# Weight combinations of q, k and v taken two neighbouring columns at a time

## The chip, the cores and the metric

The kernel runs on one core of a Trainium2 chip. The metric is the device time of one execution in microseconds (us); a kernel's time is the median of its runs. A core has TensorE (PE in the profile; PEld is its weight load), VectorE (DVE), ScalarE (ACT), GpSimd (POOL) and SyncE (SP), which here issues nearly all DMA transfers from one queue, in order.

## The reference

Two layers of attention and feed-forward run one after the other over 2048 tokens of 1024 features, with the same weights in both:

```python
x = x + attention(layernorm(x), wqkv, wo)
x = x + mlp(layernorm(x), w1, b1, w2, b2)      # and both once more

def attention(x, wqkv, wo):                     # 32 heads of 32 features
    q, k, v = split(x @ wqkv)
    idx = pos[:, None] - 2 * arange(8)          # a window of 8 tokens, every second one
    logits = sum(q * k[idx]) * scale            # positions before the start masked out
    return (softmax(logits) * v[idx]).sum() @ wo

def mlp(x, w1, b1, w2, b2):
    h = relu(x @ w1 + b1)
    return (h * h) @ w2 + b2                    # 1024 -> 3584 -> 1024
```

## The kernel before

**Tiling.** Tokens are cut into four blocks of 512 for each layer, so there are eight units, u = 0 to 7. For each unit the kernel does a LayerNorm and a transpose (SA, `ln`), the products for q, k and v (SQ or SQ7), the windowed attention on VectorE (S2), the product with wo, the residual sum and a second LayerNorm (SW), and the two products of the feed-forward (SF1, SF2). A unit's attention on VectorE runs beside matrix products of the unit before.

**Where the columns of q, k and v go.** The 1024 columns of q (and of k, and of v) are cut into eight chunks of 128. Chunk c holds columns c, c + 8, c + 16 and so on, since the attention wants each head's 32 features spread over the chunks. `SQ`, used for units 0 to 2, therefore loads its left factor (the weights) straight from the tile of wqkv with a step of eight columns (`wv[:, kd % 4, c0:D:8]`, line 710; line 715 for the few that are cut into halves of 256 tokens).

**Seven products in place of eight.** From unit 3 on, `SQ7` computes q, k and v by a scheme in which a product of two by two blocks takes seven block products and some sums in place of eight products. The blocks are halves of the 1024 input features (k), halves of the output columns (m) and halves of the 512 tokens. For each of q, k and v there are two such groups, s = 0 and 1. A group's weight blocks are chunks 4m + 2s and 4m + 2s + 1 of input half k. Three of the seven left factors are raw blocks and four are sums or differences of blocks. They are made once, in `keep_wqkv`, after unit 2 has used the raw weights (`QU = 2`), and written to device memory (`wqs`); units 3 to 7 read them from there (`seven`).

**How the left factors are made.** `raw(m, k)` is the view of one block: 4 slices of 128 input features by 2 chunks by 128 columns, 1024 elements in each partition, read with a step of eight columns. ScalarE copies three raw blocks (line 419, tiles `tr`) and VectorE makes four combinations s1 to s4 (line 424, tiles `tv`), where s2 uses s1 and s4 uses s2. Each result, a tile of 128 x 4 x 256 16-bit elements, is stored by a DMA on SP's queue (`store`). The six groups make 18 copies and 24 combinations. The same code shape without the step of eight is in `keep_w1` (line 548) for the feed-forward.

**How they are used.** `product` (lines 510 to 521) issues, for each of the two chunks a of a left factor, four matmuls of 256 tokens, whose left factor is 128 columns of the tile (line 519). The feed-forward products of `ffn1_step` call the same function. Five units with q, k and v make 42 products of 8 matmuls each, 1680 matmuls in all.

**What sets the order.** All work is first collected as operations with an engine, a price in microseconds and a priority (`Plan.add`). `Plan.schedule` then plays the execution through with these prices, and the order it finds is written out; each engine and SP's queue run their instructions in that order. A price is therefore part of the order and not of the hardware's time. An operation on 1024 elements is priced at `dve(1024, False)` = 1.14 for line 424 and `act(1024)` = 0.91 for line 419. Buffers come from pools with a fixed number of slots, so a late reader holds up a later writer.

Of the kernel before, what the change touches and what calls it, by code (L numbers as in the profile page):

```python
# [29 lines left out]
def dve(n, fast=True):  # L30
    return 0.075 + n * (0.000521 if fast else 0.00104)

def act(n):
    return 0.05 + n * 0.00084
# [171 lines left out]
class _Kernel:  # L206
# [191 lines left out]
    def keep_wqkv(self, nm, ws):  # L398

        nc, p = self.nc, self.p  # L400
        job = "k" if nm == "k" else "qv"

        def one(s):
            at = {pr: i for i, (d, pr) in enumerate(self.orderq[job]) if d == (nm, s)}

            def raw(m, k):
                return ws[k][:].rearrange("p (a b) n -> p a (b n)", a=4).rearrange("p a (n c) -> p a c n", c=8)[:, :, 4 * m + 2 * s:4 * m + 2 * s + 2, :]

            def store(pr, t, cast=None):
                i = at[pr]  # L410
                self.dma(lambda: self.wqs[job][i // 4][:, i % 4], lambda: t[:], [(t, 0)], [(("wqs", job, i // 4), i % 4)], 0.26, prio=50.0,
                         name="wqst", cast=cast, lat=4.0)

            def v4(t):
                return t[:].rearrange("p k (c n) -> p k c n", c=2)

            for pr, m, k in ((1, 0, 0), (2, 0, 1), (4, 1, 1)):
                t = Buf("2K", "tr", [128, 4, 256], BF)
                p.add("ACT", act(1024), lambda t=t, m=m, k=k: nc.scalar.copy(v4(t), raw(m, k)), [(ws[k], 0)], [(t, 0)], 30.0, name="trc")  # L419
                store(pr, t, BF)  # L420
            s1, s3, s2, s4 = t = [Buf("2K", "tv", [128, 4, 256], F16) for _ in range(4)]

            def comb(t, a, b, op, r, pr):
                p.add("DVE", dve(1024, False), lambda: nc.vector.tensor_tensor(v4(t), a(), b(), op), r, [(t, 0)], self.nxt(), name="tq")  # L424
                store(pr, t)
            comb(s1, lambda: raw(1, 0), lambda: raw(1, 1), ALU.add, [(ws[0], 0), (ws[1], 0)], 5)
            comb(s3, lambda: raw(0, 0), lambda: raw(1, 0), ALU.subtract, [(ws[0], 0)], 7)
            comb(s2, lambda: v4(s1), lambda: raw(0, 0), ALU.subtract, [(ws[0], 0), (s1, 0)], 6)
            comb(s4, lambda: raw(0, 1), lambda: v4(s2), ALU.subtract, [(ws[1], 0), (s2, 0)], 3)
        one(0)  # L430
        one(1)

    def SQ7(self, u, job):
# [36 lines left out]
    def qkv_step(self, u, nm, s):  # L470

        nc, p = self.nc, self.p
        dst = self.state[u][nm]
        off = 0 if nm == "q" else HALO
        X, Y, Z = (Buf("ps", n, [128, 2, HB], F32) for n in "XYZ")
        us = {}

        def out(m, n2):
            return dst[:, 4 * m + 2 * s:4 * m + 2 * s + 2, off + n2 * HB:off + (n2 + 1) * HB]

        def cells(m, n2):
            return [(dst, (4 * m + 2 * s + a, n2)) for a in range(2)]

        def keep(i):
            us[i] = Buf("1K", "u", [128, 2, HB], F16)
            p.add("ACT", act(512), lambda: nc.scalar.copy(us[i][:], X[:]), [(X, 0)], [(us[i], 0)], 1.0, name="u")  # L486

        def vadd(m, n2, i, bank):
            p.add("DVE", dve(512, False), lambda: nc.vector.tensor_tensor(out(m, n2), us[i][:], bank[:], ALU.add),
                  [(us[i], 0), (bank, 0)], cells(m, n2), -90.0, name="qa")  # L490

        def mul(pr, w, wi, rhs, rc):
            bank, fm = self.product(pr, w, wi, rhs, X, Y, Z)
            self.state[u]["gate" + nm] = p.add("PE", 4 * MM, fm, rc + [(w, 0)], [(bank, 0)], self.nxt(), name="fq")
            if pr == 1:
                keep(1)
            elif pr == 2:
                vadd(0, 0, 1, Y)
            elif pr == 6:
                keep(2)  # L500
            elif pr == 7:
                keep(3)
                vadd(1, 1, 3, Z)
            elif pr == 4:
                p.add("ACT", act(512), lambda: nc.scalar.copy(out(1, 0), X[:]), [(X, 0)], cells(1, 0), 2.0, name="cast")
            elif pr == 3:
                vadd(0, 1, 2, Z)
        return mul

    def product(self, pr, w, wi, rhs, X, Y, Z):  # L510
        nc = self.nc
        bank = {1: X, 6: X, 7: X, 4: X, 2: Y, 5: Z, 3: Z}[pr]
        start, raw = pr in (1, 2, 5), pr in (1, 2, 4)

        def fm():
            for a in range(2):
                for k in range(4):
                    lw = w[:, wi].bitcast(BF) if raw else w[:, wi]
                    nc.tensor.matmul(bank[:, a, :], lw[:, k, a * 128:(a + 1) * 128], rhs(k), start=(start and k == 0 and a == 0), stop=(k == 3),  # L519
                                     skip_group_check=True)  # L520
        return bank, fm

# [411 lines left out]
    def ffn1_step(self, r2, dp):  # L934
        nc, p = self.nc, self.p
        h = self.KF // 2
        f0 = 2 * dp
        X, Y, Z = (Buf("ps", nm, [128, 2, HB], F32) for nm in "XYZ")
        r1, r3 = (Buf("2K", "rr", [128, 2, 2, HB], F16) for _ in range(2))
        us = {}  # L940

        def keep(i):
            us[i] = Buf("1K", "u", [128, 2, HB], F16)
            p.add("ACT", act(512), lambda: nc.scalar.copy(us[i][:], X[:]), [(X, 0)], [(us[i], 0)], 1.0, name="u")  # L944

        def vadd(r, m, i, bank):
            y = Buf("1K", "y", [128, 2, HB], F16)
            p.add("ACT", act(512), lambda: nc.scalar.copy(y[:], bank[:]), [(bank, 0)], [(y, 0)], 1.5, name="y")  # L948
            p.add("DVE", dve(512), lambda: nc.vector.tensor_tensor(r[:, :, m, :], us[i][:], y[:], ALU.add),  # L949
                  [(us[i], 0), (y, 0)], [(r, (a, m)) for a in range(2)], -90.0, name="hc")  # L950

        def vrelu(r, a, m, f):
            ms = range(2) if m is None else (m,)
            c = [(r, (a, i)) for i in ms]
            v = (lambda: r[:, a]) if m is None else (lambda: r[:, a, m, :])
            p.add("DVE", 0.07 + len(ms) * 0.067 + 0.06, lambda: nc.vector.tensor_scalar(out=v(), in0=v(), scalar1=self.b1T[:, f:f + 1], scalar2=0.0,  # L956
                                                                                 op0=ALU.add, op1=ALU.max), c, c, -89.0, name="hr")

        def square(r, f):
            p.add("ACT", act(1024), lambda: nc.scalar.activation(out=r2[:, f:f + 2, :].rearrange("p a t -> p (a t)"),  # L960
                                                                 in_=r[:].rearrange("p a m t -> p (a m t)"), func=ACTF.Square),
                  [(r, (a, m)) for a in range(2) for m in range(2)], [(r2, (f + a, m)) for a in range(2) for m in range(2)], 1.9, name="sq")

        def mul(pr, w, wi, rhs, rc):
            bank, fm = self.product(pr, w, wi, rhs, X, Y, Z)
            self.ffs.append(p.add("PE", 4 * MM, fm, rc + [(w, 0)], [(bank, 0)], self.nxt(), name="ff"))
            if pr == 1:
                keep(1)
            elif pr == 2:
                vadd(r1, 0, 1, Y)  # L970
            elif pr == 6:
                keep(2)
            elif pr == 7:
                keep(3)
                vadd(r3, 1, 3, Z)
                for a in range(2):
                    vrelu(r3, a, 1, h + f0 + a)
            elif pr == 4:
                for a in range(2):
                    p.add("ACT", 0.36, lambda a=a: nc.scalar.activation(out=r3[:, a, 0, :], in_=X[:, a, :], func=ACTF.Relu,  # L980
                                                                            bias=self.b1T[:, h + f0 + a:h + f0 + a + 1], scale=1.0),
                          [(X, 0)], [(r3, (a, 0))], 2.0, name="relu")
                square(r3, h + f0)
            elif pr == 3:
                vadd(r1, 1, 2, Z)
                for a in range(2):
                    vrelu(r1, a, None, f0 + a)
                square(r1, f0)
        return mul
# [191 lines left out]
```

## Time and profile before

| | |
|---|---|
| time, median of 3 runs | 1203.62 us (1200.96 to 1207.49) |
| the profiled execution | 1206.54 us, of which the span of the trace is 1204.5 us |
| PE busy | 1165.5 us (97%) |
| PEld busy | 772.9 us (64%) |
| DVE busy | 1061.0 us (88%) |
| ACT busy | 742.5 us (62%) |
| line 424, combinations of q, k, v | 24 on DVE, 219.8 to 309.4 us |
| line 419, raw blocks of q, k, v | 18 on ACT, 200.3 to 294.4 us |
| line 519 for q, k, v | first at 393.0 us |

The profile gives one execution. In its rows an entry such as `128x1024 f16<-128x1024 bf16` is the shape written and the shape read, over 128 partitions. A row of the tile view gives the number of instructions, then the shortest, median and longest duration in nanoseconds, then the first and last start. In a table of stretches, each engine's busy time is followed by the number of instructions, in the order PE, PEld, DVE, ACT, POOL; then come the granted TensorE clock (1.00 is full speed), the DMA share and the GB/s moved. In a timeline a line gives the start, the length and the instructions, and in brackets the idle time before them and what ended it. A matmul's recorded duration is longer than its spacing, since matmuls overlap; the spacing is read from the starts.

### The profile page before, as it was taken

Reading aid. Unit: us, or ns where it says so; the run is one execution under the profiler, and the core shown is the slowest. Engines: PE = TensorE matmul, PEld = TensorE weight load, DVE = VectorE, ACT = ScalarE, POOL = GpSimd, SP = SyncE. Lnnn points to the kernel's source line nnn. Section 1 sums busy time; section 2 is a strip of 40 time slices with the busy share of each in tenths; the row PEclk is TensorE's granted clock in tenths of the full one; section 3 lists DMA queues with packets and bytes.
Section 4 is the critical chain, followed back from the end, with each engine's and each line's share of the span. In section 5 each row is a group of like instructions: output and inputs, shape, how many; then the busy total and the mean of one; then the engine's idle time right before and its main releaser. Section 6 shows DMA issues by size and latency. Waiting matters only on the chain.

```text
span 1204.5 us, 19912 instructions
## 1 busy us (share of the span) xinstructions
PE 1165.5 (97%) x7594; PEld 772.9 (64%) x7643; DVE 1061.0 (88%) x1737; ACT 742.5 (62%) x1355; POOL 5.0 (0%) x13
## 2 busy tenths in 40 slices
PE   7999999988799999999999999999999999999998
PEld 4665444545674688566884678646884678744863
DVE  4799999989999889996999979997999979998452
ACT  4642794388694469827596277935698275911750
POOL 1000000000000000000000000000000000000000
PEclk9999999998899999999999999999999999999999
DMA  9678999889879897997979979797979979578964
GB/s 271 201 237 252 302 328 318 288 252 289 303 237 357 311 349 281 301 380 265 375 244 354 381 239 360 268 352 273 378 272 319 392 261 344 199 276 314 347 218 154
DMA packets 199871, 356.53 MB, mean 296 GB/s; under 512 B 67424, under 2 KB 138336, under 8 KB 180576
## 3 DMA queue, kind: packets, MB, share of 16 engines
q1 hardware_dynamic: 196112, 355.25, 86.3%
q0 software_dynamic: 3664, 0.02, 0.4%
q8 instruction: 60, 0.98, 0.3%
q14 instruction: 35, 0.29, 0.1%
HBM read 307.50 MB, written 39.58 MB: 288 GB/s over the span
## 4 chain that ended last, share of the span: by engine, by line
PE 70%; DVE 5%; DMA 3%; issue 1%; ACT 0%; SPq 0%; DVEq 0%
PE X L519 20%; PE X L1022 14%; PE Z L519 11%; PE py L870 7%; PE Z L1022 7%; PE Y L519 5%; PE Y L1022 4%; DVE tv L424 1%; DVE P L773 1%; PE lg L788 1%; DMA w<-in_B_w_dram 1%; DMA w<-in_A_wo_dram 1%; DMA xt<-in_A_x_dram 1%; DVE P L781 1%; DVE T L566 0%
## 5 line engine op out<-in xcount | busy, mean ns | idle before, releaser
L519 PEld LDWEIGHTS <-w 128*128 128x128 f16 (+1 forms) x4224 | 415.4, 98 | 70.5 <-DVE T L566 6.8
L1022 PEld LDWEIGHTS <-r 128*128 128x128 f16 x1176 | 115.2, 98 | 140.1 <-issue 6.2
L1022 PE MATMUL X<-w,r 128*128 128x512 f16 (+1 forms) x775 | 175.7, 380 | 1.2 <-DMA w<-in_B_w_dram 0.8
L773 DVE TENSOR_TENSOR P<-q,k 128x2048 f16<-128x2048 f16 x128 | 154.0, 1233 | 13.8 <-ACT q L723 13.7
L834 DVE TENSOR_TENSOR pr<-pb,v 128x2048 f16<-128x2048 f16 x128 | 154.4, 1230 | 0.1
L519 PE MATMUL X<-T,w 128*128 128x256 f16 x1104 | 136.5, 274 | 0.2 <-ACT u L944 0.2
L840 DVE TENSOR_TENSOR pr<-pr 128x1024 f16<-128x1024 f16 (+1 forms) x256 | 131.7, 558 | 0.0
L486 ACT CAST u<-X 128x512 f16<-128x512 f32 x90 | 52.1, 579 | 119.7 <-PE X L519 119.7
L710 PE MATMUL pq<-xnA,w 128*128 128x512 f16 x552 | 122.6, 380 | 3.3 <-DMA w<-in_A_wqkv_dram 1.7
L781 DVE TENSOR_TENSOR P<-P,P 128x2048 f16<-128x2048 f16 x96 | 117.0, 1226 | 0.1
L870 PE MATMUL py<-w,o 128*128 128x512 bf16 x492 | 113.0, 379 | 3.4 <-ACT k L723 1.8
L944 ACT CAST u<-X 128x512 f16<-128x512 f32 x147 | 87.4, 616 | 46.2 <-PE X L519 39.6
L960 ACT ACTIVATE r<-rr 128x1024 f16<-128x1024 f16 x98 | 106.2, 1107 | 2.2 <-DVE rr L956 1.9
L710 PEld LDWEIGHTS <-w 128*128 128x128 bf16 x552 | 78.8, 144 | 43.2 <-DMA w<-in_A_wqkv_dram 2.1
L870 PEld LDWEIGHTS <-o 128*128 128x128 bf16 x512 | 50.1, 98 | 59.9 <-issue 3.2
L519 PE MATMUL X<-TA,w 128*128 128x256 f16 x720 | 86.8, 273 | 0.0
L949 DVE TENSOR_TENSOR rr<-u,y 128x512 f16<-128x512 f16 x147 | 60.2, 424 | 25.0 <-ACT y L948 20.3
L875 DVE TENSOR_TENSOR xm<-py,xt 128x512 f32<-128x512 f32 x64 | 44.4, 697 | 29.5 <-PE py L870 28.6
L948 ACT CAST y<-Z 128x512 f16<-128x512 f32 x98 | 61.0, 641 | 10.6 <-PE Z L519 10.5
L419 ACT COPY tr<-w 128x1024 bf16<-128x1024 bf16 x18 | 37.2, 2112 | 33.2 <-DMA w<-in_A_wqkv_dram 18.8
L956 DVE TENSOR_SCALAR rr<-rr,b1T 128x256 f16<-128x256 f16 (+1 forms) x196 | 51.0, 319 | 0.5
L519 PE MATMUL Z<-T,w 128*128 128x256 f16 x352 | 44.5, 280 | 5.9 <-DVE T L566 5.9
(134 smaller groups left out, 1629.4 us busy)
## 6 DMA issues: line engine op xcount, KB each, us to landing
w<-w1s SPq DMA_DIRECT2D x78, 1024.0 KB, 9.0
w<-tw SPq DMA_DIRECT2D x56, 896.0 KB, 7.2
w<-in_B_w_dram SPq DMA_DIRECT2D x42, 896.0 KB, 5.8
w<-wqqv SPq DMA_DIRECT2D x35, 1024.0 KB, 7.3
w<-in_A_wqkv_dram SPq DMA_DIRECT2D x18, 1024.0 KB, 8.2
w<-in_A_wo_dram SPq DMA_DIRECT2D x16, 1024.0 KB, 8.2
w<-wqk SPq DMA_DIRECT2D x15, 1024.0 KB, 8.3
w<-in_B_w_dram SPq DMA_DIRECT2D x28, 512.0 KB, 7.3
```

Of the source, the lines that this page charges most:

```text
L519: nc.tensor.matmul(bank[:, a, :], lw[:, k, a * 128:(a + 1) * 128], rhs(k), start=(start and k == 0 and a == 0), stop=(k == 3), skip_group_ ...
L710: nc.tensor.matmul(pq[:], wv[:, kd % 4, c0:D:8], xnT[:, :, kd, :], start=(kd == 0), stop=(kd == KD - 1))
L773: nc.vector.tensor_tensor(cur[:], q[:, c, None, hb * HB:(hb + 1) * HB].to_broadcast([128, W, HB]), _win_ap(k[:, c, :], HALO + hb * HB, HB) ...
L781: nc.vector.tensor_tensor(other[:], other[:], cur[:], ALU.add)
L834: p.add("DVE", dve(2048), lambda pr=pr, ch=ch: nc.vector.tensor_tensor(pr[:], pb[:], _win_ap(v[:, ch, :], HALO + hb * HB, HB), ALU.mult), ...
L840: nc.vector.tensor_tensor(dst, pr[:, 0:n, :], pr[:, n:2 * n, :], ALU.add)
L870: nc.tensor.matmul(py[:], o[:, c, tl * 128:(tl + 1) * 128], wos[c // 4][:].rearrange("p (a b) n -> p a (b n)", a=4)[:, c % 4, db * 512:(db ...
L944: p.add("ACT", act(512), lambda: nc.scalar.copy(us[i][:], X[:]), [(X, 0)], [(us[i], 0)], 1.0, name="u")
L948: p.add("ACT", act(512), lambda: nc.scalar.copy(y[:], bank[:]), [(bank, 0)], [(y, 0)], 1.5, name="y")
L949: p.add("DVE", dve(512), lambda: nc.vector.tensor_tensor(r[:, :, m, :], us[i][:], y[:], ALU.add), [(us[i], 0), (y, 0)], [(r, (a, m)) for a ...
L960: p.add("ACT", act(1024), lambda: nc.scalar.activation(out=r2[:, f:f + 2, :].rearrange("p a t -> p (a t)"), in_=r[:].rearrange("p a m t -> ...
L1022: nc.tensor.matmul(banks[q][:], left(jj, q), w[:, j, :], start=(start and jj == 0 and b2 is None), stop=(jj == h - 1), skip_group_check=True)
```

## The change

Inside a tile of a left factor, the 256 columns were ordered chunk by chunk: 128 columns of the first chunk and then 128 of the second. After the change they alternate: column n of the first chunk, column n of the second, and so on. Since the two chunks of a block are neighbouring columns of wqkv (4m + 2s and 4m + 2s + 1 in each group of eight), the view `raw` now reads two neighbouring columns, then jumps by eight, and the tile is written in the same order without a jump. The number of elements, of instructions, of stores and of loads is the same.

`product` gets a new argument, `left`, which picks the columns of chunk a: every second column from a for q, k and v, and the 128 columns side by side, as before, for the feed-forward. The planner's price of line 419 goes from 0.91 to 1.2 and that of line 424 from 1.14 to 1.2.

```diff
             def raw(m, k):
-                return ws[k][:].rearrange("p (a b) n -> p a (b n)", a=4).rearrange("p a (n c) -> p a c n", c=8)[:, :, 4 * m + 2 * s:4 * m + 2 * s + 2, :]
+                return ws[k][:].rearrange("p (a b) (n c) -> p a (b n) c", a=4, c=8)[:, :, :, 4 * m + 2 * s:4 * m + 2 * s + 2]
...
             def v4(t):
-                return t[:].rearrange("p k (c n) -> p k c n", c=2)
+                return t[:].rearrange("p k (n c) -> p k n c", c=2)
...
-                p.add("ACT", act(1024), lambda t=t, m=m, k=k: nc.scalar.copy(v4(t), raw(m, k)), [(ws[k], 0)], [(t, 0)], 30.0, name="trc")
+                p.add("ACT", 1.2, lambda t=t, m=m, k=k: nc.scalar.copy(v4(t), raw(m, k)), [(ws[k], 0)], [(t, 0)], 30.0, name="trc")
...
-                p.add("DVE", dve(1024, False), lambda: nc.vector.tensor_tensor(v4(t), a(), b(), op), r, [(t, 0)], self.nxt(), name="tq")
+                p.add("DVE", 1.2, lambda: nc.vector.tensor_tensor(v4(t), a(), b(), op), r, [(t, 0)], self.nxt(), name="tq")
...
         def mul(pr, w, wi, rhs, rc):
-            bank, fm = self.product(pr, w, wi, rhs, X, Y, Z)
+            bank, fm = self.product(pr, w, wi, rhs, X, Y, Z, lambda a: slice(a, 256, 2))
...
-    def product(self, pr, w, wi, rhs, X, Y, Z):
+    def product(self, pr, w, wi, rhs, X, Y, Z, left):
...
-                    nc.tensor.matmul(bank[:, a, :], lw[:, k, a * 128:(a + 1) * 128], rhs(k), start=(start and k == 0 and a == 0), stop=(k == 3),
+                    nc.tensor.matmul(bank[:, a, :], lw[:, k, left(a)], rhs(k), start=(start and k == 0 and a == 0), stop=(k == 3),
...
         def mul(pr, w, wi, rhs, rc):
-            bank, fm = self.product(pr, w, wi, rhs, X, Y, Z)
+            bank, fm = self.product(pr, w, wi, rhs, X, Y, Z, lambda a: slice(a * 128, (a + 1) * 128))
```

## The prediction

> **What bounds the kernel now.** I read the page first: busy shares, then the slices, to see which engine limits which stretch.
>
> ```profile
> PE 1165.5 (97%) x7594; PEld 772.9 (64%) x7643; DVE 1061.0 (88%) x1737; ACT 742.5 (62%) x1355; POOL 5.0 (0%) x13
> PE   7999999988799999999999999999999999999998
> PEclk9999999998899999999999999999999999999999
> ```
>
> TensorE is nearly always busy; after its start the one dent is in slices 8 to 10 (241 to 331 us). So I asked for the busy times of stretches around it.
>
> ```profile
> 240.00:270.00 30.00, 27.09 (x123) 14.79 (x124) 25.20 (x21) 24.58 (x33) 0.00 (x0) 1.00 0.82 256
> 270.00:300.00 30.00, 25.23 (x126) 17.24 (x126) 29.97 (x28) 25.96 (x39) 0.00 (x0) 0.89 0.91 280
> 300.00:330.00 30.00, 22.45 (x179) 18.30 (x177) 28.52 (x39) 18.28 (x33) 0.00 (x0) 0.83 0.86 318
> 330.00:400.00 70.00, 69.84 (x441) 43.23 (x443) 67.75 (x125) 46.27 (x87) 0.00 (x0) 1.00 0.91 306
> ```
>
> In the dent VectorE (third busy column) is full while TensorE falls to 25 and 22 of 30 us, and the granted clock drops to 0.89 and 0.83. From 330 us TensorE is full again. What VectorE does there is the tile view of the combinations' buffers, with the neighbouring rows as a yardstick.
>
> ```profile
> L548 DVE TENSOR_TENSOR tv<-w x14: 680/692/703, 88.1 to 158.6; 128x1024 f16<-128x1024 bf16 x14
> L424 DVE TENSOR_TENSOR tv<-w x12: 1993/2058/2177, 219.8 to 296.7; 128x1024 f16<-128x1024 bf16 x12
> L419 ACT COPY tr<-w x18: 2054/2098/2218, 200.3 to 292.4; 128x1024 bf16<-128x1024 bf16 x18
> ```
>
> The same operation on the same 1024 elements takes 0.69 us at L548, where columns lie side by side, and 2.06 us at L424, which reads every eighth column. The 24 combinations of L424 and the 18 copies of L419 all fall between 200 and 310 us. Last, the chain of waits over 195 to 330 us, and TensorE's timeline there:
>
> ```profile
> by line: DVE tv L424 13.2%; DVE P L773 6.2%; DMA xt<-in_A_x_dram 6.0%; issue 5.6%; DVE P L781 5.4%; PE X L519 4.6%; PE py L870 4.0%; PE Z L519 3.9%; DMA w<-w1s 3.5%; DVE xm L875 2.4%; DVE T L566 2.1%; PE lg L788 1.4%; PE Y L519 1.3%; DVE rr
> 278.77 4.00 DVE tv L424 x2
> 294.56 1.89 DVE tv L424
> 304.45 1.95 DVE tv L424
> ```
>
> ```profile
> 245.73 1.89 PE L870 MATMUL py<-w,o 128*128 128x512 bf16 x8 [1.30 <-ACT k L723]
> 270.59 17.43 PE L710 MATMUL pq<-xnA,w 128*128 128x512 f16 x80 [1.56 <-DVE xm L875]
> 293.95 3.60 PE L519 MATMUL Z<-T,w 128*128 128x256 f16 x16 [4.18 <-DVE T L566]
> 314.99 1.04 PE L788 MATMUL lg<-P,grp 128*128 128x512 f16 x2 [7.55 <-DVE P L781]
> ```
>
> L424 is the largest item of that chain, and the three long waits of TensorE (brackets: us, releaser) end on VectorE results queued behind it.
>
> **The ceiling.** From 248.15 us to 320.09 us TensorE runs 47 matmuls of L870 and 128 of L710 (0.216 us apart), 128 of L519 (0.109) and 4 of L788 (0.216): 10.1 + 27.6 + 14.0 + 0.9 = 52.6 us of work in 71.9. So 19.3 us can be won there, and 1.30 + 0.54 = 1.8 just before (two waits for ScalarE's casts): 21 us.
>
> **Part 1, the 24 combinations.** In VectorE's queue one now takes 1.94 us (two in a row start at 240.29, the next instruction at 244.16). The new price is in no row, since none reads runs of two. Bounds: 0.60 us if it goes like L548 (start to start), 1.94 if nothing changes; I exclude dearer, since the halo copy (L749) reads runs of seven, 56 elements in 0.09 us, without a price per run. Between them: contiguous rows of 512 and 1024 elements are 0.34 and 0.60 us apart, so 0.07 fixed and 0.52 ns an element. The scattered row pays (1.94 - 0.07) / 1024 = 1.83 ns for each jump of 16 bytes; with pairs it makes 512 jumps: 1.00 us. If VectorE instead takes one element a step, twice 0.52 ns: 1.13 us. I take 1.06, the middle of these two, a saving of 0.88 each.
>
> Not all 24 count. On the chain from 253.5 to 315 us I count twelve: 254.21, 265.95 and its partner (268.14, shown as issue), 271.14, 273.18 (issue), 278.77 (two), 289.53 (issue), 291.69, 294.56, 296.79, 304.45. Those of 256 to 264 lie beside an x load of 8.05 us that ends last, and the eight before 250 run while TensorE is full. 12 x 0.88 = 10.6 us.
>
> What is late next: the LayerNorms feeding the transposes. ScalarE is full from 270 to 280 (9.84 of 10) and ends the last at 279.15; the transposes sit in SP's queue behind stores that wait for combinations, so they move up too. T would then be ready near when TensorE reaches it. The wait at L788 shrinks but stays, because it is VectorE's order that ends it.
>
> **Part 2, the 18 copies on ScalarE.** 2.00 us apart now; the nearest contiguous pass, the squaring of L960, records 1.06 to 1.11. Bounds 1.0 and 2.0; the jump rule above gives about 1.05. Most lie beside other work. Three (241.16 twice, 245.56) delay the casts that TensorE awaits: 3 x 0.95 = 2.85, of which only the 1.8 of idle can be won.
>
> **Part 3, the left factors.** Each of 5 units x 42 products x 8 = 1680 matmuls in L519 now loads every second column. Loads before: 98 ns contiguous, 143 ns at a step of eight columns (L710, L715). No row has a step of two. What matters is whether a 256-column matmul still follows every 0.109 us, and the first block shows that at a step of eight:
>
> ```profile
> 14.63 2.79 PE L715 MATMUL pq<-xnA,w 128*128 128x256 f16 x24
> 17.26 0.59 PE L710 MATMUL pq<-xnA,w 128*128 128x512 f16 x2
> 396.54 1.91 PE L519 MATMUL X<-TA,w 128*128 128x256 f16 x16
> 398.28 1.91 PE L519 MATMUL Y<-xnA,w 128*128 128x256 f16 x16
> ```
>
> (17.26 - 14.63) / 24 = 0.1096 us with 143 ns loads, (398.28 - 396.54) / 16 = 0.1088 with 98 ns ones. A gain is excluded, since a contiguous load is the easiest; cost 0, the cover being the matmul before it. Where TensorE restarts after a wait, a load stands bare: up to 45 ns more, some 20 times, 0.9 us at most.
>
> [...]
>
> [...]
>
> **Part 4, the order.** The planner's prices go from 1.14 to 1.2 (L424) and 0.91 to 1.2 us (L419), so the written order shifts on every engine and on SP. Stores and loads stay as many and as large. I cost it at 0; the bound is the largest single load waits of the chain, 8.65 us (the wo load at 812.51), either way.
>
> **Sum.** -10.6 - 1.8 = -12.4, plus at most 0.9. The clock adds a little: near 294 and 315 matmuls run at half speed, about 5 us lost; I count none. From 330 us TensorE idles under 1.5% in each 100 us, so a lead won is carried to the end. The profiled execution (1206.54 us, span 1204.5) becomes 1194.5; it lies 2.9 above the median of 1203.62, so the median becomes 1191.6, said as 1192.
>
> **Rivals.**
> - Packed fully, clock kept (0.60 us): 12 x 1.34 + 1.8 + 3 of clock = 21, the ceiling: 1183. For it, L548; against it, the jumps remain.
> - DMA becomes the bound: 250 to 320 us moves 20.7 MB in 70 us. At 320 GB/s, the 300 to 330 row, that takes 65: a gain of 5, 1198. For it, a DMA share of 0.91; against it, 417 GB/s between 310 and 320.
> - Nothing gets cheaper, because short runs cost as much as jumps: 1204.
> - A new order that opens one or two load waits of 8.65 us: -12.4 + 8.65 gives 1200, with two 1208.5. For it, little slack on TensorE; against it, SP's stores finish sooner.
> - Slower: the strided loads bound the 1680 matmuls of the q, k, v products. If a long stream falls to the 143 ns that a load records, it costs 34 ns x 1680 = 57: 1249. It decides from 7.4 ns a matmul (12.4 / 1680). Only the 24 matmuls in a row speak against it.
>
> **How the numbers follow.** Forecast (gain 8 to 17) 0.50, packed 0.12, DMA 0.13, nothing cheaper 0.07, new order 0.11, strided loads 0.07. About 0.5% (6 us) is what a measurement here can tell from no change. Faster: 0.46 + 0.12 + 0.05 = 0.63; slower: 0.07 + 0.05 from orders worse than two waits + 0.02 of the forecast gone wrong = 0.14; same: 0.23. Range 1182 (the ceiling) to 1210 (two new waits); the forecast's own is 1187 to 1196.
>
> **What would show it.** Right: L424 near 1.1 us, L419 near 1.1, the waits for T and xm gone and that for P shorter, the clock near 1 in 270 to 300, L519 of the q, k, v products still 1.75 us per 16. Wrong: L424 still near 2, the waits refilled by transposes or w1 loads, or 16 matmuls taking over 1.85 us.

## The result and the profile after

The changed kernel takes 1185.09 us (median of 4 runs, 1183.00 to 1186.20) where the kernel before took 1204.82 on the same chip (1200.96 to 1207.49): a ratio of 0.9837, with a 95% interval of 0.9805 to 0.9868. In a second comparison, described below, it was 1185.40 against 1202.61, 0.9873 (0.9851 to 0.9894). The forecast was 1192, with a range of 1182 to 1210: the direction and the range held, but the gain was 17 to 20 us where 12.4 were summed, above the band of 8 to 17 that the forecast gave itself.

The dent in the page of the changed kernel is gone (line numbers after 510 are one higher than before):

```profile
PE 1160.7 (98%) x7643; PEld 769.7 (65%) x7643; DVE 1038.8 (88%) x1737; ACT 727.7 (62%) x1355; POOL 5.0 (0%) x13
PE   6999999999999999999999999999999999999998
PEclk9999999999999999999999999999999999999999
```

Busy times by stretch, in the same columns as before:

```profile
240.00:270.00 30.00, 30.00 (x141) 17.07 (x140) 22.17 (x26) 23.82 (x48) 0.00 (x0) 1.00 1.08 316
270.00:300.00 30.00, 29.72 (x217) 23.33 (x216) 29.38 (x44) 23.23 (x39) 0.00 (x0) 1.00 1.02 374
300.00:330.00 30.00, 30.00 (x257) 24.93 (x255) 29.93 (x57) 29.47 (x53) 0.00 (x0) 1.00 0.73 258
```

TensorE, 25.23 and 22.45 us busy in the last two of these before, is now busy for 29.7 and 30 us, at full clock. VectorE has 7.8 us to spare between 240 and 270. The operations that were changed, in the tile view:

```profile
L419 ACT COPY tr<-w x18: 1109/1166/1203, 198.6 to 280.4; 128x1024 bf16<-128x1024 bf16 x18
L424 DVE TENSOR_TENSOR tv<-w x12: 1069/1113/1144, 218.2 to 275.6; 128x1024 f16<-128x1024 bf16 x12
```

So 2.06 became 1.11 us on VectorE and 2.10 became 1.17 on ScalarE. And TensorE's timeline where its five waits were (the lines between 284.91 and 294.09 and between 294.09 and 324.64 have no wait and are left out):

```profile
226.16 13.98 PE L711 MATMUL pq<-xnA,w 128*128 128x512 f16 x64
239.97 13.98 PE L871 MATMUL py<-w,o 128*128 128x512 bf16 x64
253.79 27.79 PE L711 MATMUL pq<-xnA,w 128*128 128x512 f16 x128
281.42 1.91 PE L520 MATMUL X<-xnB,w 128*128 128x256 f16 x16
283.16 1.91 PE L520 MATMUL Z<-T,w 128*128 128x256 f16 x16
284.91 1.91 PE L520 MATMUL X<-T,w 128*128 128x256 f16 x16
294.09 0.60 PE L789 MATMUL lg<-P,grp 128*128 128x512 f16 x2 [0.28 <-DVE P L782]
324.64 0.38 PE L373 MATMUL X<-b2r,pick 128*128 128x512 bf16 x1
```

The waits for casts, for xm and for T have no bracket any more, and the one for P is 0.28 us where it was 7.55.

**Where the time went.** As a yardstick I take one stretch of TensorE's work: from the first product of unit 2's k (L711 at 226.16) to the first matmul with b2 of unit 1 (L373 at 324.64). It took 118.54 us before (228.72 to 347.26) and takes 98.48 now, 20.1 less. Nearly the same matmuls lie in it: the new order puts one product of 8 more ahead of its end (376 matmuls of 256 columns for 368), which is 0.9 us of work, so at equal work the difference is 20.9. The profile of before accounts for nearly all of that. These are the lines that the prediction does not show, with two stretches of 10 us:

```profile
228.72 13.98 PE L710 MATMUL pq<-xnA,w 128*128 128x512 f16 x64
248.15 10.52 PE L870 MATMUL py<-w,o 128*128 128x512 bf16 x47 [0.54 <-ACT k L723]
297.34 3.12 PE L519 MATMUL X<-T,w 128*128 128x256 f16 x16
300.30 1.91 PE L519 MATMUL Y<-xnB,w 128*128 128x256 f16 x16
315.82 1.92 PE L519 MATMUL Z<-xnB,w 128*128 128x256 f16 x8
317.53 1.06 PE L788 MATMUL lg<-P,grp 128*128 128x512 f16 x2
318.38 1.92 PE L519 MATMUL Z<-xnB,w 128*128 128x256 f16 x8
320.09 2.02 PE L519 MATMUL Z<-T,w 128*128 128x256 f16 x16
347.26 0.38 PE L373 MATMUL X<-b2r,pick 128*128 128x512 bf16 x1
```

```profile
290.00:300.00 10.00, 6.05 (x30) 4.33 (x31) 10.00 (x11) 6.12 (x9) 0.00 (x0) 0.66 0.76 285
310.00:320.00 10.00, 5.01 (x20) 2.99 (x21) 9.89 (x16) 4.35 (x9) 0.00 (x0) 0.50 1.02 417
```

The five waits in the stretch are 1.30 + 0.54 + 1.56 + 4.18 + 7.55 = 15.1 us. Behind the two long ones matmuls were spaced wider: the 32 from 293.95 took 6.35 us to 300.30 where 32 take 3.49, and the next 16 of L519 and 4 of L788, from 314.99 to 320.09, took 5.10 in place of 2.61. That is 2.9 + 2.5 = 5.3 us at a reduced clock (0.66 granted from 290 to 300, 0.50 from 310 to 320). Together 20.5, of which the wait of 0.3 is left.

The rest of the difference between the two spans (1204.5 - 1183.2 = 21.3) is 2.6 us that the changed kernel is already ahead when the stretch begins, and 1.3 that it loses behind it. The 2.6 comes from a wait near 128 us (2.09 us in the profile of before, 1.02 in that of after) and from a granted clock of 0.60 behind the longer one. The engines and SP's queue still run in the same order there, and the first changed instruction comes 70 us later, so it is no effect of the change.

### The profile page after: what moved, and what is told of

Read it like the earlier page. It is cut to its first block, busy times and chain, and to the rows that moved or that the text cites. A ratio compares the mean times of both kernels' runs of the same rounds, so it can differ in the third digit from the quotient of the medians.

```text
span 1183.2 us, 19960 instructions
## 1 busy us (share of the span) xinstructions
PE 1160.7 (98%) x7643; PEld 769.7 (65%) x7643; DVE 1038.8 (88%) x1737; ACT 727.7 (62%) x1355; POOL 5.0 (0%) x13
## 4 chain that ended last, share of the span: by engine, by line
PE 86%; DVE 7%; DMA 5%; issue 1%; ACT 1%; SPq 0%; DVEq 0%
PE X L520 20%; PE X L1023 13%; PE Z L520 10%; PE pq L711 9%; PE py L871 9%; PE Z L1023 7%; PE Y L520 5%; PE py L364 4%; PE ph L901 4%; PE Y L1023 3%; PE lg L789 2%; DMA w<-in_A_wo_dram 1%; DMA w<-in_A_wqkv_dram 1%; DVE P L774 1%; DMA w<-in_B_w_dram 1%
## 5 line engine op out<-in xcount | busy, mean ns | idle before, releaser
L1023 PEld LDWEIGHTS <-r 128*128 128x128 f16 x1176 | 115.1, 98 | 141.7 <-issue 7.7
L711 PE MATMUL pq<-xnA,w 128*128 128x512 f16 x552 | 122.5, 379 | 1.7 <-DMA w<-in_A_wqkv_dram 1.7
L711 PEld LDWEIGHTS <-w 128*128 128x128 bf16 x552 | 78.8, 144 | 41.5 <-DMA w<-in_A_wqkv_dram 2.1
L364 PE MATMUL py<-w,r 128*128 128x512 bf16 x224 | 49.7, 379 | 0.0
L1023 PE MATMUL Y<-w,r 128*128 128x512 bf16 x196 | 46.5, 388 | 2.7 <-DMA w<-in_B_w_dram 2.7
```

The lines of the kernel that those rows point to most:

```text
L364: nc.tensor.matmul(bank[:], r2[:, k2 * h + j0 + j, tl * 128:(tl + 1) * 128], w[:, k2, j, n2 * BLK:(n2 + 1) * BLK], start=False, stop=(j0 + ...
L711: nc.tensor.matmul(pq[:], wv[:, kd % 4, c0:D:8], xnT[:, :, kd, :], start=(kd == 0), stop=(kd == KD - 1))
L1023: nc.tensor.matmul(banks[q][:], left(jj, q), w[:, j, :], start=(start and jj == 0 and b2 is None), stop=(jj == h - 1), skip_group_check=True)
```

## The experiments

Each of the first four changes one thing in one of the two kernels. They ran on one chip beside the kernel before, which took 1208.60 us there; the changed kernel was not among them, so it is compared with them by ratios. "Stretch" is the yardstick above, from one profiled execution each, and that is not always a typical one: it was the slowest of ten for the prices alone (1208.36 us), the slowest of four for the combinations alone (1191.54) and one of the two slower of four for the new layout in the old order (1197.01). The order also decides whether the stretch holds 376 matmuls of 256 columns or 368: it is 376 in the changed kernel, the prices alone, the combinations alone and the copies alone.

**Prices alone.** The kernel before, with only the planner's two prices set to 1.2.

```diff
-                p.add("ACT", act(1024), lambda t=t, m=m, k=k: nc.scalar.copy(v4(t), raw(m, k)), ...
+                p.add("ACT", 1.2, lambda t=t, m=m, k=k: nc.scalar.copy(v4(t), raw(m, k)), ...
-                p.add("DVE", dve(1024, False), lambda: nc.vector.tensor_tensor(v4(t), a(), b(), op), ...
+                p.add("DVE", 1.2, lambda: nc.vector.tensor_tensor(v4(t), a(), b(), op), ...
```

> Old layout, only the planner's two prices changed to 1.2, so the written order of the changed kernel without its faster operations (nearly: the order follows the prices alone). Theory 'durations' (the 19.7 us between the medians 1204.8 and 1185.1 come from shorter combinations and copies): L424 still 2.06 us, L419 2.1, waits of TensorE between 242 and 320 us still there, 1199 to 1210 us. Rival 'order' (the 7 us beyond my forecast of 12.4 come from the new order): about 1198 us, or less.

Measured: 1202.72 against 1208.60, 0.9952 (0.9929 to 0.9975). TensorE's waits in it:

```profile
267.59 17.43 PE L710 MATMUL pq<-xnA,w 128*128 128x512 f16 x80 [1.34 <-DVE xm L875]
294.72 3.60 PE L519 MATMUL Z<-T,w 128*128 128x256 f16 x16 [7.96 <-DVE T L566]
310.87 1.04 PE L788 MATMUL lg<-P,grp 128*128 128x512 f16 x2 [3.08 <-DVE P L781]
```

The order moved waiting time from P to T and removed little: with one of 0.71 us for casts, the waits add up to 13.1 us where they were 15.1, and the stretch is 117.1 us, 1.5 less (2.3 at equal work). The whole time is 5.9 lower by the medians, between what the two theories asked for. So the order alone is worth something like 0.5% (3 to 8.5 us by the interval), and I had put it at nothing.

**The new layout in the old order.** The changed kernel with the old prices (1.14 and 0.91): the diff above, reversed, on the changed kernel.

> New layout, old prices (1.14 and 0.91), so the order of the kernel before with the faster operations. Durations: 1183 to 1188 us, L424 1.11 us, TensorE without waits over 1 us between 242 and 300. Order: about 1192 us, some of the old waits left (for T or for P).

Measured: 1192.99 (1188.60 to 1198.02), 0.9845 (0.9784 to 0.9906); stretch 104.1 us, L424 1.11 us. One wait is left in the stretch:

```profile
298.25 1.03 PE L789 MATMUL lg<-P,grp 128*128 128x512 f16 x2 [3.98 <-DVE P L782]
```

The shorter operations bring most of the gain without the new order. Whether the new order adds to them the whole times can't say, as this interval holds the changed kernel's ratio: the four runs took 1188.60, 1188.98, 1197.01 and 1198.02 us. The stretch (104.1 against 98.5) is that of one of the two slower ones. That the new order adds something is not shown.

**Combinations alone, copies alone.** Both keep the prices of 1.2. In the first only L424 works in pairs and the raw blocks are as before; in the second it is the reverse.

```diff
+            def raw_old(m, k): ...      # the view before the change
+            def v4_old(t): ...
...
-                p.add("ACT", 1.2, ... nc.scalar.copy(v4(t), raw(m, k)), ...
+                p.add("ACT", 1.2, ... nc.scalar.copy(v4_old(t), raw_old(m, k)), ...
...
-            bank, fm = self.product(pr, w, wi, rhs, X, Y, Z, lambda a: slice(a, 256, 2))
+            bank, fm = self.product(pr, w, wi, rhs, X, Y, Z, lambda a: slice(a * 128, (a + 1) * 128) if pr in (1, 2, 4) else slice(a, 256, 2))
```

> Order of the changed kernel; the 24 combinations of VectorE in pairs, the 18 copies of ScalarE in the old layout (2.1 us again), each left factor read to match. If VectorE's combinations carry the gain: 1185 to 1190 us, at most the 1.8 to 3 us of TensorE's two waits for casts lost. If the copies matter more, as they stand ahead of casts and LayerNorm pieces in ScalarE's queue: over 1193.

> The reverse: the copies in pairs (1.17 us), the combinations in the old layout (2.06 us). If the combinations carry the gain: 1199 to 1205 us, waits for T and P still there. If the copies matter: under 1197.

Measured: combinations alone 1188.20, 0.9819 (0.9777 to 0.9861), stretch 103.5; copies alone 1201.69, 0.9934 (0.9908 to 0.9960), stretch 115.1. Against the prices alone (1202.72, 117.1) the combinations bring 14.5 us and the copies 1.0, or 13.6 and 2.0 by the stretch. VectorE's combinations carry the gain; the intervals of the copies alone and the prices alone overlap, so by the whole times the copies alone bring nothing that can be told. A stretch with both is 5.0 shorter than with the combinations alone. The whole times do not show that: the ratio of the combinations alone (0.9819) is not above that of the changed kernel (0.9837 and 0.9873). So whether the copies weigh more once the combinations are short is not shown. The timeline of the combinations-alone kernel shows what they cost in that one execution:

```profile
285.14 1.92 PE L526 MATMUL Z<-T,w 128*128 128x256 f16 x16 [1.08 <-DVE T L573]
289.30 2.98 PE L526 MATMUL X<-T,w 128*128 128x256 f16 x16 [2.23 <-ACT u L951]
292.08 2.54 PE L526 MATMUL Y<-xnB,w 128*128 128x256 f16 x16
```

ScalarE, busy with 2.1 us copies, is now the one that TensorE waits for (ACT u), and behind these waits matmuls are slow again (16 in 2.78 and 2.38 us in place of 1.75; the clock granted from 270 to 300 us is 0.94, and 1.00 in the changed kernel). VectorE waits for ScalarE too, at the first of these lines; the second is a wait for a store, which the changed kernel has as well (3.56 us at 251.33):

```profile
248.48 0.18 DVE L756 COPY halo<-k 128x56 f16<-128x56 f16 x1 [4.16 <-ACT k L730]
256.00 1.13 DVE L430 TENSOR_TENSOR tv<-w,tv 128x1024 f16<-128x1024 bf16 x1 [2.55 <-DMA wqk<-tv]
```

**Which combinations count.** The prediction counted 12 of 24 and held the eight for k, before 250 us, to be free. Four kernels test that. They form a family of their own, compared only within itself: all LayerNorm outputs are transposed by TensorE and copied out by VectorE, in place of DMA transposes (`on_pe=True` in both calls of `ln`); all keep the prices of 1.2. One has the old layout, one pairs for k, one pairs for q and v, one pairs throughout.

```diff
             def raw(m, k):
+                if nm != "k":        # the kernel with pairs for k alone
+                    return ...       # the view before the change
                 return ws[k][:].rearrange("p (a b) (n c) -> p a (b n) c", a=4, c=8)[:, :, :, 4 * m + 2 * s:4 * m + 2 * s + 2]
```

> A second family, in which every LayerNorm output is transposed by TensorE and copied out by VectorE, in place of the DMA transposes. This one: old layout, planner's prices of 1.2. TensorE gains 52 transposes of 8 matmuls (about 52 x 0.45 = 23 us by the row of L658) and VectorE 52 copies: 1220 to 1250 us, with waits behind L424 between 240 and 320 us as in the kernel before. It is the base for the three that follow.

> Same family and prices; pairs for the weights of k alone: the 8 combinations before 250 us and 6 copies. The prediction's count holds these 8 for free, as TensorE is full while they run: then as p_none, within 2 us. Rival: VectorE's lateness is handed on to the waits after 260 us, so 8 x 0.92 = 7.4 less than p_none.

> Same family and prices; pairs for the weights of q and v alone: 16 combinations, 12 copies. By the prediction's count the whole gain of the family (p_none less p_all) lies here. Rival: two thirds of it, 16 x 0.92 = 14.7 where p_all has 22.

> Same family and prices; all in pairs, the changed kernel with TensorE's transposes. 12 to 22 us less than p_none: 12 if only those on the chain of the kernel before count, 22 (24 x 0.92) if all do. Matmuls of the q, k, v products 1.75 us per 16 with the step of two.

Measured on one chip: 1230.44 without pairs, 1228.20 with pairs for k, 1217.77 with pairs for q and v, 1213.28 with all. So k brings 2.2 us, q and v 12.7, all 17.2 (4.5 of it for k on top of q and v). The 12.7 are three quarters of the whole gain, nearer to the rival's two thirds than to all of it. In VectorE's timeline of the kernel with k alone, the 7.4 us that its eight combinations save come back as waits (8.4 us in these three; without pairs, none of the three is over 0.3):

```profile
248.31 2.03 DVE L427 TENSOR_TENSOR tv<-w 128x1024 f16<-128x1024 bf16 x1 [2.13 <-DMA wqqv<-tr]
254.39 0.18 DVE L753 COPY halo<-k 128x56 f16<-128x56 f16 x1 [4.05 <-ACT k L727]
265.24 1.99 DVE L427 TENSOR_TENSOR tv<-w 128x1024 f16<-128x1024 bf16 x1 [2.24 <-DMA wqqv<-tv]
```

Two of them end with a store (DMA wqqv<-tr, wqqv<-tv): the combination could not start before an earlier buffer had been written out. TensorE's waits in the stretch, the first two lines without pairs and the last two with pairs for k:

```profile
268.67 2.17 PE L658 MATMUL pt<-ident,xn 128*128 128x128 f16 x16 [3.84 <-ACT xn L583]
317.79 1.03 PE L788 MATMUL lg<-P,grp 128*128 128x512 f16 x2 [9.03 <-DVE P L781]
```

```profile
269.88 2.17 PE L662 MATMUL pt<-ident,xn 128*128 128x128 f16 x16 [4.84 <-ACT xn L587]
318.77 1.04 PE L792 MATMUL lg<-P,grp 128*128 128x512 f16 x2 [7.35 <-DVE P L785]
```

With pairs for k, TensorE even gets past the wait for P 1 us later. From the first product of unit 2's k to the first matmul with b2, the four kernels take 116.5 us without pairs, 117.2 with pairs for k, 104.8 for q and v and 101.1 for all, with the same matmuls in each. So in the stretch k alone brings nothing, q and v bring 11.7 and all 15.4. The 2.2 us of k in the whole times arise behind the stretch, and their cause stays open. The prediction's view of these eight holds as long as q and v are slow. Once these are short, k is worth 3.7 us in the stretch (4.5 in the whole times), and that the count did not have. TensorE has no wait for the casts of k in the stretch of this family.

**Loads at a step of eight.** The pairs-throughout kernel of that family, with the 1680 left factors read at a step of eight columns across the tile, so the output is another; the work is the same.

```diff
-                    nc.tensor.matmul(bank[:, a, :], lw[:, k, left(a)], rhs(k), ...
+                    nc.tensor.matmul(bank[:, a, :], lw.rearrange("p k n -> p (k n)")[:, 2 * k + a:1024:8], rhs(k), ...
```

> The changed kernel with TensorE's transposes; the 1680 left factors of the q, k, v products from unit 3 on are loaded with a step of eight columns (16 bytes) across the tile, so they hold other columns than the reference's; the work is the same. Prediction's reading of L715 (a 143 ns load does not slow a 256-column matmul, even in a long stream): 16 matmuls still 1.75 us. Rival 'loads bound the stream': 16 matmuls 2.29 us (143 ns each), 57 us more; anything over 1.80 us per 16 speaks for it in part.

The tile view of this kernel's loads between 371 and 396 us, and its timeline:

```profile
L520 PEld LDWEIGHTS <-w x108: 140/143/148, 382.4 to 395.9; 128*128 128x128 f16 x60, 128*128 128x128 bf16 x48
```

```profile
382.59 1.91 PE L520 MATMUL X<-xnA,w 128*128 128x256 f16 x16
384.34 1.91 PE L520 MATMUL Z<-TA,w 128*128 128x256 f16 x16
386.08 1.91 PE L520 MATMUL X<-TA,w 128*128 128x256 f16 x16
```

The loads take 143 ns, as in L715, and 16 matmuls still take 1.75 us. The changed kernel itself, at a step of two, has the same spacing with loads of 98 ns (the view of line 520 between 371 and 381 us, and its timeline):

```profile
L520 PEld LDWEIGHTS <-w x90: 97/98/98, 371.1 to 380.9; 128*128 128x128 f16 x48, 128*128 128x128 bf16 x42
```

```profile
371.29 1.91 PE L520 MATMUL X<-xnA,w 128*128 128x256 f16 x16
373.04 1.91 PE L520 MATMUL Z<-TA,w 128*128 128x256 f16 x16
```

The one run at a step of eight took 1213.57 us, on another chip than the 1213.28 for the same kernel at a step of two; their stretches are 101.0 and 101.1 us. So loads that record 143 ns still let the matmuls follow each other every 0.109 us (1.75 / 16), and the rival of the strided loads, 57 us, is refuted at a step of two and of eight.

**Six patterns of reading.** The same kernel, in which the six groups read their 1024 elements in six patterns and so hold other columns; sizes and writes are the same.

```diff
             def raw(m, k):
-                return ws[k][:].rearrange("p (a b) (n c) -> p a (b n) c", a=4, c=8)[:, :, :, 4 * m + 2 * s:4 * m + 2 * s + 2]
+                f = ws[k][:].rearrange("p (a b) n -> p a (b n)", a=4)
+                if g == 1:                       # runs of 4 every 16 bytes; one such case for each group
+                    return f.rearrange("p a (n c) -> p a n c", c=8)[:, :, 0:64, 4 * m:4 * m + 4]
...
```

> The changed kernel with TensorE's transposes; the six groups of combinations and copies read 1024 elements in six patterns, so they hold other columns than the reference's: k, s=0: runs of 2 every 16 bytes (as the change); k, s=1: runs of 4 every 16; q, s=0: one run side by side; q, s=1: runs of 2 every 8 bytes; v, s=0: runs of 4 every 32; v, s=1: single columns every 4 bytes. On VectorE, by 'a jump to another 16 bytes costs 1.83 ns, else paired': 1.1, 0.69, 0.69, 0.69, 0.69 and 1.2 us. By 'short runs go one element a step': 1.1 to 1.2 for every group but the third, 0.69 there. On ScalarE, by the jumps: 1.1 in all six; singles no dearer.

One line of VectorE's timeline for each of the six, in the order of the expectation:

```profile
231.02 1.09 DVE L438 TENSOR_TENSOR tv<-tv,w 128x1024 f16<-128x1024 f16 x1
241.79 0.69 DVE L438 TENSOR_TENSOR tv<-tv,w 128x1024 f16<-128x1024 f16 x1
249.20 0.68 DVE L438 TENSOR_TENSOR tv<-tv,w 128x1024 f16<-128x1024 f16 x1
265.59 0.68 DVE L438 TENSOR_TENSOR tv<-tv,w 128x1024 f16<-128x1024 f16 x1
271.65 0.69 DVE L438 TENSOR_TENSOR tv<-tv,w 128x1024 f16<-128x1024 f16 x1
280.26 1.22 DVE L438 TENSOR_TENSOR tv<-tv,w 128x1024 f16<-128x1024 f16 x1
```

And the 18 copies of ScalarE, all patterns together:

```profile
L433 ACT COPY tr<-w x18: 1039/1064/1155, 204.7 to 285.2; 128x1024 bf16<-128x1024 bf16 x18
```

Every one of VectorE's six is within 0.02 us of what was expected by the jump rule, which is an estimate. Runs of two take 0.68 us when they follow every 8 bytes, as one run side by side does, and 1.09 when they follow every 16 bytes, so it is not the short run that costs here, but where the next one lies. Singles every 4 bytes take 1.22, where 1.2 was expected. The kernel took 1210.78 us in its one run, on another chip than the family; its stretch is 99.0 us where that with pairs throughout is 101.1, so a shorter combination is worth little by now.

**Truer prices, and the changed kernel again.** The changed kernel with prices of 1.02 and 1.08, close to what its operations take, beside the changed kernel itself.

> The changed kernel with the planner's prices set to what the operations take in its queue, 1.02 for L424 and 1.08 for L419, in place of 1.2. If the order matters only through prices that are far off: as the changed kernel, within 0.3%. If a truer price gives a better order: up to 5 us less, since the last waits of the stretch are already gone, hardly more.

> The changed kernel itself, beside the others on one chip: 0.9837 of the kernel before, within 0.3%. It is the measure for e11_true_prices and, through the kernel before, for the new layout in the old order (0.9845) and the combinations alone (0.9819).

Measured: 1189.59 (1186.11 to 1191.68), 0.9882, and 1185.40 (1184.49 to 1191.50), 0.9873: not told apart. In its profile, one of its slower executions (1190.84 us), the truer prices have the longer stretch (104.1 against 99.9 us), with waits of 1.97 us for T and 2.92 for P. That a price nearer to the hardware's makes a better order is not shown here. No kernel is told apart as faster than the changed one.

## Why the prediction was right, and where it was off

**The bound** was right: the dent was VectorE's, and with the combinations alone shortened, 14.5 us of the time went.

**Part 1, the price** was right: 1.06 was taken, and two in a row are now 1.025 us apart in VectorE's queue (2.05 us from 234.93 to the next instruction at 236.98; 1.94 before, so 0.92 saved by each). The jump rule gave 1.00 and the single step 1.13, and the middle was taken without a reason for either, so that it fell so near is partly luck. Both were estimates, the second with a factor of two that no run had shown. The six patterns agree with the jump rule, and single columns every 4 bytes are 1.13 us from start to start there (280.26 to 281.39), twice 0.52 ns an element. VectorE's queue in the changed kernel:

```profile
234.93 2.17 DVE L424 TENSOR_TENSOR tv<-w 128x1024 f16<-128x1024 bf16 x2
236.98 1.32 DVE L1077 TENSOR_TENSOR xo<-py,xm 128x512 bf16<-128x512 f32 x2
```

**Part 1, the count.** "12 x 0.88 = 10.6": the combinations alone brought 13.6 us in the stretch. About 3.6 of these are matmuls at a slow clock, and TensorE's waits fell from 13.1 to 3.3 us, by 9.8, or eleven combinations at 0.92. So the size of the count was near; its reason, that the eight for k are free, held only while q and v were slow (in the other family). The shortfall of the sum is mainly the clock: "about 5 us lost; I count none". Of the 20.1 us by which the stretch is shorter, 14.8 are waits, where 12.4 were summed, and with the waits the reduced clock went, 5.3 us (1.00 is granted from 240 to 330 us now). I had seen it and left it out of the sum; it belonged in it, since both waits ahead of it were among those I expected to shrink. (The 1194.5 of the prediction's sum is 0.4 above 1206.54 - 12.4; that does not matter here.)

**Part 2** fits alone: 1.8 were taken, the stretch gives 2.0, and the whole times can't tell it from nothing. In company it may be too small: with the combinations short, the stretch with the copies is 5.0 us shorter (3.5 against the second profile of the changed kernel, whose stretch is 99.9), but by one slow execution of the combinations alone, and the whole times do not bear it out. I priced the copies only against TensorE's waits of before, and not against one that the shorter combinations uncovered in that execution: ACT u.

**"The wait at L788 shrinks but stays"** was too cautious: of 7.55 us only 0.28 is left, 1.73 in the second profile. VectorE reached the last sum ahead of L788 18.3 us earlier, counted from the stretch's start: 23 combinations from there on shorten its queue by 21 us, only 3.5 us come back as idle time, and the new order has one sum fewer ahead of it. For this wait nearly all combinations count, not twelve.

**Part 3** was right: loads at a step of two take 98 ns, as side by side, and the products 1.75 us per 16. To go by the row of L715 was right, and now for a long stream too. That nothing at all is lost even at a step of eight is more than the 24 matmuls of L715 could show.

**Part 4, the order,** "I cost it at 0", was off by about 6 us in the old layout: alone it gave 0.9952. The three orders of the new layout differ by up to 5.6 us in the stretch, in one execution each; their whole times are not told apart. What part of the changed kernel's gain is its order stays open within these bounds.

Of the rivals, full packing did not happen (1.11, not 0.69), though its time, 1183, was nearly reached; the stretch came close to the ceiling of 21 us another way, by nearly all waits going and the slow clock with them. DMA did not become the bound: it moved 374 GB/s from 270 to 300 us.

## What to carry to other kernels

Look at one duration per shape: the elementwise operation that took three times its neighbour's time on the same shape (2.06 us for 0.69) was the one that read single columns, and pairs nearly halved it here (1.11), as whoever reads the result could take a step. Sum a stall with the slow clock that follows it (here 15.1 us of waits and 5.3 behind two of them), and, for each wait that goes, look for the next engine in line as it will be then. An order written from prices moves with each price, and that alone was as large here (0.5%) as what a measurement could tell. A profile is one execution: before a difference of two profiles is believed, see where their executions lie among the runs.

## What the runs showed of the hardware that was not expected

- A 128-column weight load that records 143 ns (step of 16 bytes) let 256-column matmuls follow each other every 0.109 us (80 of them from 382.59 to 391.32 us), the same as one of 98 ns. With 1680 such loads in five units the execution took 1213.57 us, and 1213.28 with loads of 98 ns. So what a load records was not the time by which the matmuls were spaced.
- Two waits of 1.08 and 2.23 us within 6 us were followed by matmuls at about two thirds of their speed (16 in 2.78 us for 1.75), so here a clock loss came without a wait of 4 us. It came behind a single wait too: in the kernel before, 2.09 us near 128 us was followed by 8 matmuls of 512 columns in 2.87 us for 1.73, at a granted clock of 0.60, while 1.87 us at the same place in the kernel with the prices alone was not (8 in 1.73).
